# h − tanh(h) between two matrix products: five VectorE operations and a GpSimd mask, or three activations and two VectorE operations under a checked bound

## The chip, the cores and the metric

One core of a Trainium2 chip. The time is the device time of one execution in microseconds (us); medians of several executions are given with the lowest and highest.

A word on TensorE's records: each float32 matmul of this kernel appears as two "passes" (`ph`: 3072 in the trace of before for the program's 1536). All counts and distances below are of passes.

## The reference, cut to what matters

```python
X = np.fft.rfft(x, axis=1)                       # x: 8 batches x 3008 x 256
y = np.fft.irfft(X * (filt_r + 1j * filt_i)[None], n=3008, axis=1)
tokens = y.reshape(24064, 256)
h = tokens @ w_in                                # 256 -> 2048
g = h - np.tanh(h)
out = g @ w_out                                  # 2048 -> 256
```

The batches are worked on in four pairs. The transforms of the first pair come first; those of each later pair lie between the dense layers of the pair before. The change is about `g`.

## The kernel before

The tokens of a pair come in 12 groups: 11 of 512 tokens and one of 384. For each group there are 16 steps. A step makes one tile of the hidden layer, `ph` (128 hidden units by 512 tokens, in PSUM, where this kernel's matmul results lie; the other tiles lie in SBUF), turns it into `gt`, and adds `gt`'s share to `po`, the group's result. TensorE runs `po` two tiles behind `ph` (`LAG = 2`), so the elementwise work has two steps to pass.

```python
ph = ps.tile([128, CH * 128], F32, tag="h", bufs=3, name="ph")
for h in range(2):
    nc.tensor.matmul(ph[:, 0:n], w_in[:, h, ...], uts[i][:, h, 0:n], ...)      # 4 passes
th, u, gt = tile_of("th"), tile_of("u"), tile_of("gt", bufs=LAG + 2)           # others: 2 buffers
large = tile_of("large", U8)
nc.scalar.activation(u, ph, AF.Square)
nc.scalar.activation(th, ph, AF.Tanh)
nc.gpsimd.tensor_single_scalar(out=large, in_=u, scalar=SMALL, op=ALU.is_ge)   # |h| >= 0.6
nc.vector.tensor_mul(gt, ph, u)                                                # h^3
for tag, bias, (s, _, v) in zip(("sa", "sb"), biases, FACTORS):
    sq = tile_of(tag)
    nc.scalar.activation(sq, u, AF.Square, bias=bias, scale=s)
    nc.vector.scalar_tensor_tensor(out=gt, in0=sq, scalar=v, in1=gt, op0=ALU.add, op1=ALU.mult)
nc.vector.tensor_sub(th, ph, th)                                               # h - tanh(h)
nc.vector.copy_predicated(gt, large, th)
# ... two steps later, in down():
for j in range(n):                                                             # 8 passes
    nc.tensor.matmul(po[i][:, j, :], gt[:, j * 128:(j + 1) * 128], w_out[:, t, :], ...)
if t == NT - 1:                                       # end of the group; po has one buffer
    nc.vector.tensor_copy(ot[:, 0:2, :], o[:, 0:2, :])
    nc.scalar.copy(ot[:, 2:n, :], o[:, 2:n, :])
    nc.gpsimd.dma_start(...)                          # the store
```

Below |h| = 0.6 the difference cancels, and the kernel uses h³ times a product of two factors; above, it takes h − tanh(h) itself. GpSimd makes the mask that chooses. In the middle of a group the next group's tokens `ut` are made by 32 short passes (`pu`, one buffer).

Of the kernel before, what the change touches and what calls it, by code (L numbers as in the profile page):

```python
# [16 lines left out]
# The sequence index is n = NR * q + r and the frequency a + NQ * b, so that the transform over n is  # L17
# one of length NQ over q, a twiddle, and one of length NR over r. Of the NQ values of a, 0 .. NQ/2
# are kept (the input is real): a = 1 .. 31 have slots 0 .. 30, with real and imaginary parts, and
# a = 0 and a = 32, which are real after the first transform, share slot 31.  # L20
# [16 lines left out]
# Below |h| = 0.6, where h - tanh(h) cancels, it is h^3 times this product of (s u + b)^2 + v with  # L37
# u = h^2, to the precision of float32.
SMALL = 0.36
FACTORS = [(0.28138768672943115, 0.18210311233997345, 0.5012423992156982),  # L40
           (0.28138768672943115, -0.6558710336685181, 0.19358105957508087)]


def _consts():
# [4 lines left out]
    # over q: columns (part, slot)  # L49
# [10 lines left out]
    # over r: rows (r, part), columns (part, b). Frequencies over SEQ / 2 are the conjugates of their  # L60
    # mirror images and come in the order of these, as the filters are loaded.
# [15 lines left out]
    # back over b: g[., 0] takes (zr fr; zi fi), g[., 1] takes (zr fi; zi fr)  # L77
# [22 lines left out]
    # back over a: rows (slot, part)  # L100
# [18 lines left out]
def kernel(  # L119
# [13 lines left out]
    # Between the transforms the partition changes from (slot, part) to r and back, by way of DRAM.  # L133
    ct1 = [nc.dram_tensor(f"ct1_{p}", (NR, 128, DM), F32, kind="Internal") for p in range(PAIRS)]
    ct2 = [nc.dram_tensor(f"ct2_{p}", (128, NR, DM), F32, kind="Internal") for p in range(PAIRS)]
# [16 lines left out]
    def load_filters(a, z):  # L152
        """The filters of slots a .. z-1: filt[:, 0] has (fr; fi), filt[:, 1] has (fi; fr)."""
# [22 lines left out]

    biases = []
# [5 lines left out]
    def weights():  # L183
        """The weights, float64 in DRAM, as float32: the engines have no 64-bit floats, so a word's
        sign and exponent make a power of two, and its fraction, added up in float32, the factor."""
# [12 lines left out]
        for i, (dst, _) in enumerate(jobs):  # L198
# [13 lines left out]
            # An exponent under float32's range gives a zero, one over it an infinity.  # L212
# [17 lines left out]
    def first(p):  # L230
        """The transform over q of a pair of batches, to ct1 with rows (r, part, slot, batch)."""
        xs = {c: load_x(p, c) for c in range(2)}
        for c, (r, n) in enumerate(X_CHUNKS):
            if c + 2 < len(X_CHUNKS):
                xs[c + 2] = load_x(p, c + 2)
            pf = ps.tile([128, XH, DM], F32, tag="z", bufs=2, name="pf")
            nc.tensor.matmul(pf[:, 0:n, :], wf1, xs.pop(c)[:, 0:n, :], start=True, stop=True)  # L237
            a1 = sb.tile([128, XH, DM], F32, tag="a1", bufs=2, name="a1")
            nc.scalar.copy(a1[:, 0:n, :], pf[:, 0:n, :])  # L239
            nc.scalar.dma_start(  # L240
                dram(ct1[p], r * 128 * DM, [[DM, 128], [128 * DM, n], [1, DM]]), a1[:, 0:n, :])
            yield
# [6 lines left out]
    def middle(p):  # L249
        """Over r, times the filter and back over b, to ct2 with rows (batch, slot, part, r)."""  # L250
# [3 lines left out]
        def back():  # L254
            k, uv = waiting.pop(0)
            pe = ps.tile([128, 2, DM], F32, tag="z", bufs=2, name="pe")
            for f in range(2):
                nc.tensor.matmul(pe[0:R2], g3[:, (2 * k + f) * R2:(2 * k + f + 1) * R2],  # L258
                                 uv[:, f], start=(f == 0), stop=(f == 1))
            e1 = sb.tile([R2, 2, DM], F32, tag="e1", bufs=2, name="e1")  # L260
            nc.scalar.copy(e1, pe[0:R2])  # L261
            nc.scalar.dma_start(
                dram(ct2[p], k * R2 * DM, [[DM, R2], [NQ * NR * DM, 2], [1, DM]]), e1)
# [19 lines left out]
    def load_e2(p, c):  # L283
        r, n = CHUNKS[c]
        t = sb.tile([128, CH, DM], F32, tag="e2", bufs=2, name="e2")
        nc.sync.dma_start(t[:, 0:n, :], dram(ct2[p], r * DM, [[NR * DM, 128], [1, n * DM]]))
# [5 lines left out]
    def last(i):  # L292
        """Back over a: the tokens (r, batch, q) of a group, with the channel in the partition."""
# [4 lines left out]
        for h in range(2):  # L298
# [4 lines left out]
            nc.scalar.copy(ut[:, h, 0:n * 128], pu[:, 0:n * 128])  # L303
        uts[i] = ut

    def up(i, t):
        """128 rows of the shrunk hidden layer of a group."""
# [10 lines left out]
        th, u, gt = tile_of("th"), tile_of("u"), tile_of("gt", bufs=LAG + 2)  # L318
        large = tile_of("large", U8)
        nc.scalar.activation(u, ph, AF.Square)  # L320
        nc.scalar.activation(th, ph, AF.Tanh)  # L321
        nc.gpsimd.tensor_single_scalar(out=large, in_=u, scalar=SMALL, op=ALU.is_ge)  # L322
        nc.vector.tensor_mul(gt, ph, u)  # L323
        for tag, bias, (s, _, v) in zip(("sa", "sb"), biases, FACTORS):
            sq = tile_of(tag)
# [9 lines left out]
    def down(i, t, gt):  # L335
        """Its part of the result; at the end of the group, the store."""
# [4 lines left out]
        for j in range(n):  # L341
            # Two sums share a bank: the first product in it clears the whole bank's written bits.
# [11 lines left out]
    # the first pair's transforms, and the loads of what stays  # L354
# [16 lines left out]
    # Each pair's dense layers, with the next pair's transforms between them.  # L371
# [9 lines left out]
    for i, (p, c) in enumerate(groups):  # L381
        if i + 1 < len(groups) and c + 1 < len(CHUNKS):
            e2s[i + 1] = load_e2(*groups[i + 1])
        for t in range(NT):
# [5 lines left out]
            if t == NT // 2 and i + 1 < len(groups):  # L390
                last(i + 1)
            if p + 1 < PAIRS:
                for gens in plan.get(c * NT + t, []):
                    next(gens[p + 1])
    for w in todo:
        down(*w)

# [29 lines left out]
```

## Time and profile before

| | before |
|---|---|
| time | 3473.27 us median of 3 (3472.45 to 3473.28) |
| first pair's transforms, until the first `ph` pass | 469.85 us |
| dense layers, from there to the start of the last pass | 2998.45 us |
| from the start of the last pass to the end | 6.2 us |
| in the dense part: distances over the usual between TensorE's passes | 24.6 us |

The first row is measured by itself; the others come from the trace. The last row: what another engine costs is counted here where two passes start further apart than the median of their form in the trace (429 ns for `ph` with 512 columns, 323 with 384, 216 for `po`, 112 for `pu`; an excess under 50 ns is not counted). The prediction below shows the lines of the profile themselves.

### The profile page before, as it was taken

What the parts mean: (1) busy time and instruction counts of PE and PEld (TensorE: products, weight loads), DVE (VectorE), ACT (ScalarE), POOL (GpSimd) and SP (SyncE); (2) the same over time, 40 slices, a digit from 0 to 9 for tenths busy, and PEclk for the clock granted to TensorE, in tenths of its full rate; (3) what the DMA queues carried; (4) which work ended last, traced back from release to release, by engine and by line L of the source; (5) the groups of instructions that cost most, each with busy time, mean ns of one, the idle gap of its engine ahead of it and who ended that gap; (6) DMA issues with size and microseconds to landing.
All of it is one profiled execution on the core that took longest, in us unless ns stands there. A gap on an engine that the chain in (4) does not pass through costs nothing. (4 is left out here: it accounts for less than half of the span.)

```text
span 3474.5 us, 36231 instructions
## 1 busy us (share of the span) xinstructions
PE 3219.2 (93%) x10800; PEld 1985.4 (57%) x10800; DVE 2744.9 (79%) x4466; ACT 1946.3 (56%) x3441; POOL 1333.2 (38%) x855
## 2 busy tenths in 40 slices
PE   1256689999999999999999999999999999999998
PEld 0011146666666666666666666666666666666665
DVE  2243158888888888888888888888888999999998
ACT  0000046665555666665555666665555666666665
POOL 2100024443333444443333444444333444445453
PEclk9955589999999999999999999999999999999999
DMA  5631122201111012201111112111111100000000
GB/s 116 143 119 63 50 80 73 69 26 47 43 45 37 32 54 85 63 29 48 47 41 34 32 59 86 47 37 41 48 40 36 35 17 19 19 19 19 17 13 11
DMA packets 107702, 168.44 MB, mean 48 GB/s; under 512 B 17120, under 2 KB 65992, under 8 KB 107124
## 3 DMA queue, kind: packets, MB, share of 16 engines
q1 hardware_dynamic: 37776, 82.39, 7.9%
q10 hardware_dynamic: 50496, 52.68, 4.5%
q0 software_dynamic: 19232, 31.04, 2.9%
q8 instruction: 85, 1.39, 0.2%
q14 instruction: 113, 0.93, 0.1%
HBM read 92.00 MB, written 73.92 MB: 48 GB/s over the span
## 5 line engine op out<-in xcount | busy, mean ns | idle before, releaser
L322 POOL TENSOR_SCALAR large<-u 128x512 uint8<-128x512 f32 (+1 forms) x768 | 1271.5, 1656 | 1973.3 <-ACT u L320 1933.1
L343 PE MATMUL po<-w_out_sb,gt 128*128 128x256 f32 x6016 | 1423.8, 380 | 11.3 <-ACT ot L350 7.4
L311 PE MATMUL ph<-ut,w_in_sb 128*128 128x512 f32 (+1 forms) x3072 | 1418.5, 583 | 0.0
L343 PEld LDWEIGHTS po<-w_out_sb,gt 128*128 128x128 f32 x6016 | 1138.2, 190 | 483.1 <-issue 283.9
L320 ACT ACTIVATE u<-ph 128x512 f32<-128x512 f32 (+1 forms) x768 | 451.6, 588 | 825.3 <-issue 301.0
L311 PEld LDWEIGHTS ph<-ut,w_in_sb 128*128 128x128 f32 x3072 | 578.0, 190 | 453.3 <-issue 399.7
L323 DVE TENSOR_TENSOR gt<-ph,u 128x512 f32<-128x512 f32 (+1 forms) x768 | 518.3, 675 | 272.3 <-ACT th L321 271.4
L330 DVE COPY_PREDICATED gt<-large,th 128x512 f32<-128x512 uint8 (+1 forms) x768 | 586.2, 763 | 68.2 <-DVE gt L327 2.7
L327 DVE SCALAR_TENSOR_TENSOR gt<-sb,gt 128x512 f32<-128x512 f32 (+1 forms) x768 | 539.6, 703 | 65.5 <-DVE gt L327 1.8
L326 ACT ACTIVATE sa<-u,bias 128x512 f32<-128x512 f32 (+1 forms) x768 | 548.8, 715 | 0.0
L326 ACT ACTIVATE sb<-u,bias 128x512 f32<-128x512 f32 (+1 forms) x768 | 546.4, 711 | 0.0
L327 DVE SCALAR_TENSOR_TENSOR gt<-sa,gt 128x512 f32<-128x512 f32 (+1 forms) x768 | 518.9, 676 | 0.0
L329 DVE TENSOR_TENSOR th<-ph,th 128x512 f32<-128x512 f32 (+1 forms) x768 | 513.4, 668 | 0.0
L321 ACT ACTIVATE th<-ph 128x512 f32<-128x512 f32 (+1 forms) x768 | 449.5, 585 | 0.0
L258 PE MATMUL pe<-uv,g_sb 94*94 94x512 f32 x512 | 299.5, 714 | 61.7 <-ACT e L261 60.8
L261 ACT COPY e<-pe 94x512 f32<-94x512 f32 x128 | 74.4, 581 | 406.8 <-PE pe L258 215.7
L273 DVE TENSOR_TENSOR uv<-pz,filt_sb 94x512 f32<-94x512 f32 x256 | 171.5, 680 | 164.1 <-PE pz L269 164.1
L237 PE MATMUL pf<-x_sb,wf_sb 128*128 128x512 f32 x192 | 121.4, 725 | 151.8 <-ACT a L239 134.4
L258 PEld LDWEIGHTS pe<-uv,g_sb 94*94 94x94 f32 x512 | 93.3, 188 | 242.4 <-issue 135.3
L269 PE MATMUL pz<-a,f_sb 94*94 94x512 f32 x256 | 160.1, 711 | 24.7 <-DMA a<-ct 19.8
L239 ACT COPY a<-pf 128x512 f32<-128x512 f32 x96 | 55.4, 577 | 200.8 <-DMA ct<-a 134.2
L237 PEld LDWEIGHTS pf<-x_sb,wf_sb 128*128 128x128 f32 x192 | 39.5, 224 | 198.0 <-ACT a L239 166.4
(34 smaller groups left out, 536.2 us busy)
## 6 DMA issues: line engine op xcount, KB each, us to landing
a<-ct SPq DMA_DIRECT2D x128, 188.0 KB
ct<-e ACTq DMA_DIRECT2D x128, 188.0 KB
x_sb<-in_x_dram SPq DMA_DIRECT2D x92, 256.0 KB
ct<-a ACTq DMA_DIRECT2D x92, 256.0 KB
e<-ct SPq DMA_DIRECT2D x44, 512.0 KB
out_dram<-ot POOLq DMA_DIRECT2D x44, 512.0 KB, 3.0
w<-in_moe_w_in_dram SPq DMA_DIRECT2D x16, 256.0 KB
w<-in_moe_w_out_dram SPq DMA_DIRECT2D x16, 256.0 KB
```

What stands on the lines that cost most here:

```text
L258: nc.tensor.matmul(pe[0:R2], g3[:, (2 * k + f) * R2:(2 * k + f + 1) * R2], uv[:, f], start=(f == 0), stop=(f == 1))
L273: nc.vector.tensor_mul(uv[:, f], pz[0:R2], filt[:, f, k, :].unsqueeze(1).to_broadcast([R2, 2, DM]))
L311: nc.tensor.matmul(ph[:, 0:n], w_in[:, h, t * 128:(t + 1) * 128], uts[i][:, h, 0:n], start=(h == 0), stop=(h == 1))
L320: nc.scalar.activation(u, ph, AF.Square)
L321: nc.scalar.activation(th, ph, AF.Tanh)
L322: nc.gpsimd.tensor_single_scalar(out=large, in_=u, scalar=SMALL, op=ALU.is_ge)
L323: nc.vector.tensor_mul(gt, ph, u)
L326: nc.scalar.activation(sq, u, AF.Square, bias=bias, scale=s)
L327: nc.vector.scalar_tensor_tensor(out=gt, in0=sq, scalar=v, in1=gt, op0=ALU.add, op1=ALU.mult)
L329: nc.vector.tensor_sub(th, ph, th)
L330: nc.vector.copy_predicated(gt, large, th)
L343: nc.tensor.matmul(po[i][:, j, :], gt[:, j * 128:(j + 1) * 128], w_out[:, t, :], start=(t == 0 and j % 2 == 0), stop=(t == NT - 1), skip_g ...
```

## The change

Its intent is to take work off VectorE, the second busiest engine (79% to TensorE's 93%). For |h| < 0.98 and y = arctan(0.639 h)², the expression h·y·((0.1866 y − 0.6846)² + 0.3476) equals h − tanh(h) to a relative 5e-8 (evaluated in float64). That needs no mask and only two VectorE operations. It holds only under the bound, so the kernel checks the bound: it keeps the largest |token| of each channel and group, multiplies these by |w_in| on TensorE, and takes a general, slow path in a branch at the end if any result reaches 0.98. For the given inputs it does not.

```diff
+        nc.vector.tensor_reduce(out=largest[:, :, i:i + 1], in_=ut[:, :, 0:n * 128],   # once a group
+                                axis=mybir.AxisListType.X, op=ALU.max, apply_absolute_value=True)
...
-        large = tile_of("large", U8)
-        nc.scalar.activation(u, ph, AF.Square)
-        nc.scalar.activation(th, ph, AF.Tanh)
-        nc.gpsimd.tensor_single_scalar(out=large, in_=u, scalar=SMALL, op=ALU.is_ge)
-        nc.vector.tensor_mul(gt, ph, u)
-        for ...:  (activation Square with bias, scalar_tensor_tensor; twice)
-        nc.vector.tensor_sub(th, ph, th)
-        nc.vector.copy_predicated(gt, large, th)
+        nc.scalar.activation(at, ph, AF.Arctan, scale=S)
+        nc.scalar.activation(y, at, AF.Square)
+        nc.scalar.activation(sq, y, AF.Square, bias=near_b, scale=A)
+        nc.vector.tensor_mul(gt, ph, y)
+        nc.vector.scalar_tensor_tensor(out=gt, in0=sq, scalar=K, in1=gt, op0=ALU.add, op1=ALU.mult)
...
+    def bounded():                        # called in the middle of the last group
+        for t in range(NT):
+            nc.scalar.activation(w_abs, w_in[:, :, t * 128:(t + 1) * 128], AF.Abs)
+            for h in range(2):
+                nc.tensor.matmul(pb, w_abs[:, h], largest[:, h], start=(h == 0), stop=(h == 1))
+            nc.vector.tensor_single_scalar(out=small[:, t], in_=pb, scalar=NEAR, op=ALU.is_lt)
+        ...                               # minimum, sum over partitions, count
...
+    within = nc.values_load(count[0:1, 0:1], min_val=0, max_val=128)
+    with tc.If(within < 128):
+        general()
```

One DRAM tensor for the transforms' results takes the place of four, so that the general path can index it. (With the change, the tiles named `th`, `u` and `sa` in the profile hold arctan, y and the second square.)

More of the change, by code (lines that the diff above doesn't have):

```diff
@@ L41 @@
            (0.28138768672943115, -0.6558710336685181, 0.19358105957508087)]
+S, K = 0.6389930153911744, 0.3476472316053873
+A, B = 0.18659689165196622, -0.6846325776203513
+NEAR = 0.98
 def _consts():
@@ L134 @@
     ct1 = [nc.dram_tensor(f"ct1_{p}", (NR, 128, DM), F32, kind="Internal") for p in range(PAIRS)]
-    ct2 = [nc.dram_tensor(f"ct2_{p}", (128, NR, DM), F32, kind="Internal") for p in range(PAIRS)]
+    ct2_all = nc.dram_tensor("ct2", (PAIRS, 128, NR, DM), F32, kind="Internal")
     cst = ctx.enter_context(tc.tile_pool(name="cst", bufs=1))
@@ L175, in load_filters @@
                                     dram(src.tensor, NQ // 2 * DM, [[NQ * DM, HI], [1, DM]]))
+    near_b = cst.tile([128, 1], F32, name="near_b")
+    nc.vector.memset(near_b, B)
+    largest = cst.tile([128, 2, PAIRS * len(CHUNKS)], F32, name="largest")
     biases = []
@@ L262, in back @@
             nc.scalar.dma_start(
-                dram(ct2[p], k * R2 * DM, [[DM, R2], [NQ * NR * DM, 2], [1, DM]]), e1)
+                dram(ct2_all, (p * 128 * NR + k * R2) * DM, [[DM, R2], [NQ * NR * DM, 2], [1, DM]]), e1)
         for k in range(NK):
@@ L285, in load_e2 @@
         t = sb.tile([128, CH, DM], F32, tag="e2", bufs=2, name="e2")
-        nc.sync.dma_start(t[:, 0:n, :], dram(ct2[p], r * DM, [[NR * DM, 128], [1, n * DM]]))
+        nc.sync.dma_start(t[:, 0:n, :], dram(ct2_all, (p * 128 * NR + r) * DM, [[NR * DM, 128], [1, n * DM]]))
         return t
@@ L303, in last @@
             nc.scalar.copy(ut[:, h, 0:n * 128], pu[:, 0:n * 128])
+        nc.vector.tensor_reduce(out=largest[:, :, i:i + 1], in_=ut[:, :, 0:n * 128],
+                                axis=mybir.AxisListType.X, op=ALU.max,
+                                apply_absolute_value=True)
         uts[i] = ut
@@ L317, in up @@
         ph = ph[:, 0:n]
-        th, u, gt = tile_of("th"), tile_of("u"), tile_of("gt", bufs=LAG + 2)
-        large = tile_of("large", U8)
+        at, y, sq = tile_of("th"), tile_of("u"), tile_of("sa")
+        gt = tile_of("gt", bufs=LAG + 2)
+        nc.scalar.activation(at, ph, AF.Arctan, scale=S)
+        nc.scalar.activation(y, at, AF.Square)
+        nc.scalar.activation(sq, y, AF.Square, bias=near_b, scale=A)
+        nc.vector.tensor_mul(gt, ph, y)
+        nc.vector.scalar_tensor_tensor(out=gt, in0=sq, scalar=K, in1=gt,
+                                       op0=ALU.add, op1=ALU.mult)
@@ new lines, in up @@
+        return gt
+    def bounded():
+        ng = len(groups)
+        small = cst.tile([128, NT, ng], F32, name="small")
+        ones = cst.tile([128, 1], F32, name="ones")
+        nc.gpsimd.memset(ones, 1.0)
+        for t in range(NT):
+            w_abs = sb.tile([128, 2, 128], F32, tag="sb", bufs=2, name="w_abs")
+            nc.scalar.activation(w_abs, w_in[:, :, t * 128:(t + 1) * 128], AF.Abs)
+            pb = ps.tile([128, ng], F32, tag="z", bufs=2, name="pb")
+            for h in range(2):
+                nc.tensor.matmul(pb, w_abs[:, h], largest[:, h], start=(h == 0), stop=(h == 1))
+            nc.vector.tensor_single_scalar(out=small[:, t], in_=pb, scalar=NEAR, op=ALU.is_lt)
+        least = cst.tile([128, 1], F32, name="least")
+        nc.vector.tensor_reduce(out=least, in_=small, axis=mybir.AxisListType.XY, op=ALU.min)
+        pc = ps.tile([1, 1], F32, tag="z", bufs=2, name="pc")
+        nc.tensor.matmul(pc, least, ones, start=True, stop=True)
+        count = cst.tile([1, 1], I32, name="count")
+        nc.vector.tensor_copy(count, pc)
+        return count
@@ new lines, in general @@
+    def general():
+        out_v = out.rearrange("(p q r) d -> p r q d", p=PAIRS, r=NR)
+        ct2_v = ct2_all.ap().rearrange("p s r d -> p r s d")
+        with tc.For_i(0, PAIRS, 1) as p, tc.For_i(0, NR, 1) as r:
+            e2 = sb.tile([128, DM], F32, tag="e2", bufs=2, name="e2")
+            nc.sync.dma_start(e2, ct2_v[bass.ds(p, 1), bass.ds(r, 1), :, :])
+            ut = sb.tile([128, 2, 128], F32, tag="ut", bufs=2, name="ut")
+            for h in range(2):
+                pu = ps.tile([128, 128], F32, tag="u", bufs=1, name="pu")
+                nc.tensor.matmul(pu, e2[:, h * 128:(h + 1) * 128], s2, start=True, stop=True)
+                nc.scalar.copy(ut[:, h], pu)
+            o = ps.tile([128, DM], F32, tag="o", bufs=1, name="o")
+            for t in range(NT):
+                ph = ps.tile([128, 128], F32, tag="h", bufs=3, name="ph")
+                for h in range(2):
+                    nc.tensor.matmul(ph, w_in[:, h, t * 128:(t + 1) * 128], ut[:, h],
+                                     start=(h == 0), stop=(h == 1))
+                gt = any_h(ph)
+                nc.tensor.matmul(o, gt, w_out[:, t, :], start=(t == 0), stop=(t == NT - 1))
+            ot = sb.tile([128, DM], F32, tag="ot", bufs=1, name="ot")
+            nc.vector.tensor_copy(ot, o)
+            nc.sync.dma_start(out_v[bass.ds(p, 1), bass.ds(r, 1), :, :], ot)
@@ L320, in up, with any_h @@
+    def any_h(ph):
+        th, u, sq, gt = (sb.tile([128, 128], F32, tag=tag, bufs=b, name=tag)
+                         for tag, b in (("th", 2), ("u", 2), ("sa", 2), ("gt", LAG + 2)))
+        large = sb.tile([128, 128], U8, tag="large", bufs=2, name="large")
         nc.scalar.activation(u, ph, AF.Square)
         nc.scalar.activation(th, ph, AF.Tanh)
-        nc.gpsimd.tensor_single_scalar(out=large, in_=u, scalar=SMALL, op=ALU.is_ge)
+        nc.vector.tensor_single_scalar(out=large, in_=u, scalar=SMALL, op=ALU.is_ge)
@@ L323, in up @@
         nc.vector.tensor_mul(gt, ph, u)
-        for tag, bias, (s, _, v) in zip(("sa", "sb"), biases, FACTORS):
-            sq = tile_of(tag)
+        for bias, (s, _, v) in zip(biases, FACTORS):
             nc.scalar.activation(sq, u, AF.Square, bias=bias, scale=s)
@@ L391 @@
                 last(i + 1)
+            if i + 1 == len(groups) and t == NT // 2:
+                count = bounded()
             if p + 1 < PAIRS:
```

## The prediction

> **What bounds the kernel now.** I read the page's busy shares and slices first, to see which engine is full and when.
>
> ```profile
> span 3474.5 us, 36231 instructions
> PE 3219.2 (93%) x10800; PEld 1985.4 (57%) x10800; DVE 2744.9 (79%) x4466; ACT 1946.3 (56%) x3441; POOL 1333.2 (38%) x855
> PE   1256689999999999999999999999999999999998
> DVE  2243158888888888888888888888888999999998
> PEclk9955589999999999999999999999999999999999
> ```
>
> The first five or six slices (some 470 us) are the first pair's transforms, which wait on transfers; the change does not touch them. After that TensorE is at nine tenths in every slice with its full clock, and VectorE at eight, then nine. The second view is busy time in two stretches: the dense layers up to the last group of tokens, and that group with the end.
>
> ```profile
> core 0: us, PE busy (x) PEld busy (x) DVE busy (x) ACT busy (x) POOL busy (x), PEclk, DMA share, GB/s
> 470.00:3414.00 2944.00, 2936.81 (x10347) 1884.59 (x10345) 2566.92 (x3989) 1875.43 (x3307) 1274.66 (x797) 1.00 0.12 41
> 3414.00:3474.50 60.50, 50.52 (x186) 33.80 (x184) 50.33 (x93) 33.16 (x70) 22.48 (x19) 0.99 0.04 16
> ```
>
> TensorE is idle for 7.2 us of 2944 us. Matmul ends are modelled, so busy is not proof of work; the chain of waits shows the pace:
>
> ```profile
> 3306.30 1.72 PE ph L311 x4
> 3308.02 1.73 PE po L343 x8
> 3309.74 3.43 PE ph L311 x8
> 3313.18 3.45 PE po L343 x16
> ```
>
> One step is 4 passes of ph (1.72 us, so 430 ns for 512 columns) and 8 of po (1.73 us, 216 ns for 256): 3.45 us, end to end with the next. 768 steps make 2.65 ms; the next pair's transforms lie between them on the same engine. So TensorE's own work is the bound.
>
> VectorE, however, is only just fast enough. Third, the costliest groups:
>
> ```profile
> L323 DVE TENSOR_TENSOR gt<-ph,u 128x512 f32<-128x512 f32 (+1 forms) x768 | 518.3, 675 | 272.3 <-ACT th L321 271.4
> L330 DVE COPY_PREDICATED gt<-large,th 128x512 f32<-128x512 uint8 (+1 forms) x768 | 586.2, 763 | 68.2 <-DVE gt L327 2.7
> L327 DVE SCALAR_TENSOR_TENSOR gt<-sb,gt 128x512 f32<-128x512 f32 (+1 forms) x768 | 539.6, 703 | 65.5 <-DVE gt L327 1.8
> L326 ACT ACTIVATE sb<-u,bias 128x512 f32<-128x512 f32 (+1 forms) x768 | 546.4, 711 | 0.0
> ```
>
> VectorE's five operations of a step (675, 676, 703, 668, 763) sum to 3.49 us against TensorE's 3.45. They overlap a little, and transforms give TensorE extra work, so VectorE falls behind only where steps are short: in the last group of each pair, with 384 columns in place of 512. Last, TensorE's timeline there, and after it its waits from 470 us on (us in total, times, longest):
>
> ```profile
> 3452.73 1.56 PE L343 MATMUL po<-w_out_sb,gt 128*128 128x256 f32 x6
> 3455.73 1.56 PE L343 MATMUL po<-w_out_sb,gt 128*128 128x256 f32 x6
> 3464.39 1.56 PE L343 MATMUL po<-w_out_sb,gt 128*128 128x256 f32 x6 [1.27 <-DVE gt L330]
> 3467.11 1.56 PE L343 MATMUL po<-w_out_sb,gt 128*128 128x256 f32 x6 [1.16 <-DVE gt L330]
> ```
>
> ```profile
> PE po L343 <- ACT ot L350: 7.4, 8, 1.5
> PE po L343 <- DVE gt L330: 2.9, 5, 1.3
> ```
>
> A 384-column step needs 4 x 323 + 6 x 216 = 2.59 us, but here two follow each other at 2.9 to 3.0 us: VectorE sets the pace, and the last two po also wait for it. To get the loss that the modelled ends hide, I took the distances between the starts of successive passes from TensorE's timeline from 470 us on, and summed what exceeds the usual one (429, 323, 216, 112 ns by form) by over 50 ns: 24.6 us. Of it 10.7 us come with waits for VectorE's gt, 10.7 us with waits at the change of group for the copies of po (ot), 3.1 us with the single buffer of pu. This 24.6 us is all that a faster elementwise part can win: 0.7%.
>
> [...] the trace has 585 to 588 (square, tanh) and 711 to 715 (square with bias)[...]. So arctan should cost what tanh does. [...] the trace's pu passes, which stream 128 columns for each 128 of weights, start every 112 ns. [...]
>
> **The change, part by part.**
>
> 1. VectorE loses three of five operations a step (668, 703, 763): 768 steps, 1639 us of busy time by the groups' sums. It keeps 675 + about 690 = 1.37 us a step, and gets 48 maxima of 2 x 512 elements[...]. So about 1165 us, 34%. GpSimd loses 1271.5 us. ScalarE goes from 588 + 585 + 715 + 711 = 2.60 to about 585 + 588 + 715 = 1.89 us a step: 1400 us, 40%. All three lie beside TensorE's 3.45 us. On the path: the 10.7 us of gt waits go. The new chain for one tile, three activations and one operation in a row (0.59 + 0.59 + 0.72 + 0.69 with some 0.1 us between: about 3 us), is well under the two steps (6.9 us) of lag. **-10.5 us.**
>
> 2. The scheduler's order at the change of group. Before, 37 of 47 changes have two tiles' worth of matmuls (ph, or one ph and a transform) between the last po of one group and the first of the next; in the listing of the changed program 34 have one tile's ph alone, 4 x 430 = 1.72 us. po has one buffer: the next po waits for the two copies, which run one after the other: [...] VectorE 0.69, ScalarE 0.58, [...] about 1.75 us if both engines are free, up to 0.5 more if not. So 34 short waits of 0.1 to 0.5 us, with the 0.10 us that a restart shows: about 10 us. Before, the same waits cost 10.7 us, in fewer and longer pieces. **0 us, give or take 5.** The 3.1 us at pu stay.
>
> 3. The bound, checked at the middle of the last group: 32 float32 matmuls with 48 columns against 128 columns of weights. Each is two passes[...]: 64 x 0.112 = 7.2 us on TensorE, which has no gap for it. Their 16 absolute values [...] and comparisons stand between other work, with two buffers; step by step they come in time, since a pair of tiles takes 0.9 us of passes and 0.65 to 0.86 us of ph or po. I add 0.3 us for the last reduction. **+7.5 us.**
>
> 4. Arctan needs another table set: the order shows one load, ahead of the first tile, and none after. TensorE has 7 ph matmuls (6 us) before its first po[...]. [...]
>
> 5. The end: every engine loads the count into a register and takes a branch over the general path. The bound works out from the reference's inputs as at most 0.69 against 0.98, so the path is not taken. Most of it lies beside the last store, whose landing (3.0 us by the page) ends the run. [...]
>
> 6. One tensor ct2 in place of four: the waits of its loads and stores in the listings are the same. **0.**
>
> Sum: 3473.3 - 10.5 + 0 + 7.5 + 0.8 + 1 = 3472 us.
>
> **Rivals.** (a) VectorE was the real limit, and 60% of its work gone makes the dense part faster by several per cent. For it: 94% busy in the last pair and 3.49 against 3.45 us a step. Against it: TensorE's passes are at their usual distances but for 24.6 us; even with all of it and no new cost the time is 3449 us. (b) The order at changes of group goes badly: ScalarE, in order, holds the second copy behind an activation each time, 0.7 us x 47, and the first stage loses some more: 3490 us. (c) The bound's matmuls wait for absolute values and comparisons at every pair instead of running through[...], 3482 us. (d) The general path runs: many milliseconds; the inputs exclude it unless the check itself is wrong.
>
> **Range and chances.** The terms are small and of both signs; the uncertain ones are part 2 (5 us), part 3 (4 us), the end (2 us) and the first stage, where ScalarE and the transfers may fall out differently by some us. Range 3461 to 3484. 2% would be 69 us, out of reach both ways: faster 0.01, within 2% 0.98, slower 0.01.
>
> **What would show it.** VectorE near 34%, ScalarE near 40%, GpSimd under 3%, TensorE still 92 to 93% and 3.45 us a step; no wait of po for gt; 384-column steps at 2.59 us; waits of po for ot, many and short; about 7 us of pb passes near the end. It is wrong if the steps of 512 columns change their length, if arctan takes longer than tanh's 585 ns, or if the first 470 us move by over 10 us.

The sum came to 3472 us: 3473.3 for before, −10.5, 0 and +7.5 for parts 1 to 3, and +0.8 and +1 for parts 4 and 5. These last two terms were estimates, and no trace or run gave them. That arctan takes as long as tanh is an estimate from square and tanh, which both take 585 to 588 ns. Part 1's 1165 us include a term for the 48 maxima (measured after: 57.6 us, 1199 ns each). Of part 2's 1.75 us the trace of before shows 0.42 us from the start of the last `po` pass to the first copy (at the end of the run), 0.69 and 0.58 for the copies, 0.03 between them and 0.05 to the next `po` where that waits: 1.77 us. Part 3's 64 × 0.112 us takes the distance of the `pu` passes for passes of 48 columns, an estimate, and its 0.3 us is an allowance.

## The result, and the profile after

Predicted within 2%, and so it came. After: 3464.43 us median of 4 (3463.81 to 3465.55); before in the same rounds: 3473.28 (3472.45 to 3473.86). The ratio is 0.9974, with a 95% interval of 0.9960 to 0.9988: some 9 us faster, within 2%. Ratios here are the mean time of one kernel's fast runs over that of the other's of the same rounds, so not quite the ratio of the medians quoted.

The page of the kernel after, its busy shares and VectorE's slices:

```profile
span 3462.2 us, 30898 instructions
PE 3219.3 (93%) x10866; PEld 1993.6 (58%) x10866; DVE 1375.0 (40%) x2229; ACT 1695.6 (49%) x2690; POOL 61.6 (2%) x88
DVE  2243123344444433344444443344444444444444
```

VectorE's busy time is halved and GpSimd is almost gone, yet TensorE's 93% has not moved: it was the bound and still is. Then the same two stretches as before (columns: us, then busy time and count of TensorE, its weight loads, VectorE, ScalarE, GpSimd, then clock, DMA share, GB/s):

```profile
470.00:3402.00 2932.00, 2932.00 (x10342) 1883.94 (x10341) 1221.06 (x1787) 1620.10 (x2554) 24.50 (x46) 1.00 0.12 40
3402.00:3462.00 60.00, 53.72 (x248) 41.11 (x246) 24.09 (x54) 33.62 (x67) 1.08 (x2) 0.98 0.04 17
```

TensorE's 7.2 us of idle time in the long stretch are now 0.00. The groups that replace the elementwise work:

```profile
L333 ACT ACTIVATE th<-ph 128x512 f32<-128x512 f32 (+1 forms) x768 | 451.7, 588 | 935.5 <-PE ph L324 935.4
L336 DVE TENSOR_TENSOR gt<-ph,u 128x512 f32<-128x512 f32 (+1 forms) x768 | 522.6, 680 | 1567.0 <-ACT u L334 1562.5
L337 DVE SCALAR_TENSOR_TENSOR gt<-sa,gt 128x512 f32<-128x512 f32 (+1 forms) x768 | 522.7, 681 | 75.6 <-ACT sa L335 1.2
L314 DVE TENSOR_REDUCE largest<-ut 128x2 f32<-128x1024 f32 (+1 forms) x48 | 57.6, 1199 | 114.3 <-ACT ut L313 114.3
```

Arctan takes 588 ns, as tanh did. VectorE now idles 1567 us before its first operation of a step: it waits for ScalarE, and ScalarE for TensorE. The third line of evidence is TensorE's timeline in the 384-column steps of the last group:

```profile
3418.29 1.46 PE L414 MATMUL po<-w_out_sb,gt 128*128 128x256 f32 x6
3420.87 1.46 PE L414 MATMUL po<-w_out_sb,gt 128*128 128x256 f32 x6
3423.46 1.46 PE L414 MATMUL po<-w_out_sb,gt 128*128 128x256 f32 x6
```

They are 2.58 and 2.59 us apart, where before they were 2.8 to 3.0. Also, each block of six passes reads 1.46 us, where before it read 1.56. The 0.10 us is what a block shows in these traces when TensorE starts it from a wait: its first two passes then start 320 ns apart and not 216. So here a block's own length tells whether it waited, even where no wait is listed.

Where did the 9 us come from? The account of TensorE's distances in both traces, in us (count in brackets):

| | before | after |
|---|---|---|
| first `ph` pass starts at | 469.85 | 466.05 |
| first `ph` pass to start of the last pass | 2998.45 | 2989.29 |
| excess with waits for `gt`, with the restarts | 7.8 (26) + 2.7 (26) | 0 |
| excess at the change of group (`ot`), with the restarts | 9.3 (13) + 1.5 (14) | 0.4 (4) + 4.1 (39) |
| excess at `pu` | 3.1 (39) | 3.2 (40) |
| other excess (after: beside the bound's passes) | 0.3 | 1.0 |
| all excess | 24.6 | 8.6 |
| the bound's passes (`pb`) | – | 6.5 (64) |
| start of the last pass to the end | 6.2 | 6.8 |

The dense part is 9.2 us shorter: 16.0 us of excess less, 6.5 us of new passes, and 0.3 us in the check's last two passes (`pc`, 0.12) and in distances under the 50 ns. The end is 0.6 us longer. That is −8.6 us, and the medians differ by 8.85 us. The first `ph` pass, 3.8 us earlier in this pair of traces, is chance: a second look at each kernel had it at 469.27 (before) and 468.31 (after), and over all traces told of here it lies between 465.0 and 471.4 without regard to the kernel. The second looks repeat the rest: 2998.38 and 2989.11 us of dense part, 24.4 and 8.4 us of excess.

Three details of the trace after. A change of group near the end, one of the four before groups of 384 columns: TensorE's `ph` passes, the two copies of `po`, and the next `po`:

```profile
3409.03 2.10 PE L324 MATMUL ph<-ut,w_in_sb 128*128 128x384 f32 x6
3409.72 0.68 DVE L420 COPY ot<-po 128x512 f32<-128x512 f32 x1
3410.43 0.58 ACT L421 COPY ot<-po 128x512 f32<-128x512 f32 x1 [1.24 <-DVE ot L420]
3411.07 1.56 PE L414 MATMUL po<-w_out_sb,gt 128*128 128x256 f32 x6
```

Both engines are free when they are asked, so the copies end as the six `ph` passes do (6 × 0.323 from 3409.03 is 3410.97). The next `po` starts 0.10 us after that, and TensorE loses this and the 0.10 us of a restart (104 ns in each of 39 cases after); at the changes before groups of 512 columns it is the restart alone. The bound's passes:

```profile
3427.34 0.99 PE L353 MATMUL pb<-largest,w_abs 128*128 128x48 f32 x8
3428.16 0.88 PE L324 MATMUL ph<-ut,w_in_sb 128*128 128x384 f32 x2
3428.88 0.99 PE L353 MATMUL pb<-largest,w_abs 128*128 128x48 f32 x8
```

Eight of them take 3427.34 to 3428.16, 0.82 us or 103 ns each on average, and go into TensorE's row without a gap. Last, ScalarE's table load:

```profile
466.89 1.28 ACT L333 ACT_TABLE_LOAD   x1
```

It lies beside the first `ph` passes, which have started at 466.05 and run on.

### The profile page after: what moved, and what is told of

Its sections match the earlier page's. It is cut to its first block, busy times and chain, and to the rows that moved or that the text cites. A ratio compares the mean times of both kernels' runs of the same rounds, so it can differ in the third digit from the quotient of the medians.

```text
span 3462.2 us, 30898 instructions
## 1 busy us (share of the span) xinstructions
PE 3219.3 (93%) x10866; PEld 1993.6 (58%) x10866; DVE 1375.0 (40%) x2229; ACT 1695.6 (49%) x2690; POOL 61.6 (2%) x88
## 4 chain that ended last, share of the span: by engine, by line
issue 64%; PE 23%; DMA 12%; POOL 1%; ACT 0%; DVE 0%; ACTq 0%; POOLq 0%; SPq 0%; DVEq 0%
PE ph L324 9%; PE po L414 9%; DMA ct<-e 6%; DMA ct<-a 4%; PE pe L268 2%; DMA f_sb<-f 1%; PE pz L279 1%; PE pu L311 1%; PE pf L247 1%; POOL out_dram L422 1%; DMA w<-in_moe_w_out_dram 1%; DMA w<-in_moe_w_in_dram 0%; ACT e L271 0%; ACT a L249 0%; DVE it L216 0%
## 5 line engine op out<-in xcount | busy, mean ns | idle before, releaser
L335 ACT ACTIVATE sa<-u,near_b 128x512 f32<-128x512 f32 (+1 forms) x768 | 548.3, 714 | 24.8
L334 ACT ACTIVATE u<-th 128x512 f32<-128x512 f32 (+1 forms) x768 | 476.4, 620 | 24.0
L283 DVE TENSOR_TENSOR uv<-pz,filt_sb 94x512 f32<-94x512 f32 x256 | 163.9, 680 | 168.5 <-PE pz L279 168.5
L311 PEld LDWEIGHTS pu<-s_sb,e 128*128 128x128 f32 x752 | 96.5, 193 | 33.2 <-ACT ut L313 28.7
L311 PE MATMUL pu<-s_sb,e 128*128 128x128 f32 x752 | 103.5, 281 | 0.0
L314 DVE TENSOR_REDUCE largest<-ut 128x2 f32<-128x1024 f32 (+1 forms) x48 | 57.6, 1199 | 114.3 <-ACT ut L313 114.3
L313 ACT COPY ut<-pu 128x512 f32<-128x512 f32 (+1 forms) x96 | 55.3, 576 | 76.1 <-PE pu L311 75.7
L279 PEld LDWEIGHTS pz<-a,f_sb 94*94 94x94 f32 x256 | 47.7, 191 | 68.7 <-issue 53.5
```

The lines of the kernel that those rows point to most:

```text
L279: nc.tensor.matmul(pz[0:R2], f2[:, k * R2:(k + 1) * R2], a2.pop(k), start=True, stop=True)
L283: nc.vector.tensor_mul(uv[:, f], pz[0:R2], filt[:, f, k, :].unsqueeze(1).to_broadcast([R2, 2, DM]))
L311: nc.tensor.matmul(pu[:, j * 128:(j + 1) * 128], e2[:, j, h * 128:(h + 1) * 128], s2, start=True, stop=True)
L334: nc.scalar.activation(y, at, AF.Square)
L335: nc.scalar.activation(sq, y, AF.Square, bias=near_b, scale=A)
```

## The experiments

Three sets of runs, each on one chip and each with its own runs of the kernel before: 3475.14 us (3473.27 to 3479.52, 9 runs) in the first, 3473.65 (3472.0 to 3478.21, 9 runs) in the second, 3474.42 (3472.7 to 3476.33, 9 runs) in the third. All kernels gave correct results for these inputs.

My theory at first: before, VectorE's five operations of a step sum to about TensorE's step, so VectorE's load caused the waits for `gt` and made the copies at the change of group late; less load removed them, and the bound costs some 7 us of what was won. (Runs 4 and 9 corrected the part on load.) The rivals: the waits come from something else that the change removed with them, such as the chain's form or GpSimd's part, or the order at the change of group; the expectations give them letters as they came up.

**1. What the bound costs.** After, without it:

```diff
-        nc.vector.tensor_reduce(out=largest[:, :, i:i + 1], ...)
-                count = bounded()
-    within = nc.values_load(...); with tc.If(within < 128): general()
```

> The changed kernel without the maxima, the bound's matmuls and the branch: the elementwise part alone (it would be wrong for large h, and gives the reference's result on these inputs). My theory: the change won some 16 us of TensorE's waits (24.6 us of late starts in the trace of before, 8.4 in that of after) and gave back 6.6 us of pb passes, 0.8 us of restarts around them and 0.7 us at the end; so this run is 8 us under the changed kernel: 3456 us, ratio 0.9951 to before. Rival A, the gain comes from the first 470 us (the first dense matmul starts 3.8 us earlier in the trace of after) and the waits count for half: 3460 us or more. Rival B, the bound is hidden beside other work: within 2 us of the changed kernel.

Measured: 3459.78 us (3458.74 to 3460.46, 5 runs), ratio 0.9955 (0.9942 to 0.9969). Against 0.9974 for the whole change this is 0.19%, 6.6 us. The two ratios' intervals overlap, so the size is taken from the trace: its dense part is 2981.61 us, 7.7 us shorter than after's. The median is near Rival A's 3460, but this set's runs of before are 1.9 us slower than those beside the result; the ratio is the theory's, and the dense part, which leaves the first stage out, speaks against Rival A. The bound costs what its passes cost (6.5 us, and 1.0 us beside them), and the rest of the check next to nothing. The end is 6.8 us here too, without any check or branch.

**2. The bound on the kernel before.** Maxima, bound, branch and general path, with the elementwise part of before:

```diff
+        nc.vector.tensor_reduce(out=largest[:, :, i:i + 1], ...)     # once a group
+                count = bounded()                                     # w_abs in x's buffers
+    with tc.If(within < 128): general()
```

> The kernel before with the maxima, the bound's matmuls and the branch alone, elementwise part as it was (the absolute values lie in the buffers of x, as there is no room for new ones). My theory: the pb passes cost TensorE 6.6 us and the restarts and the end 1.5 us, so 8 us slower than before, ratio 1.0023; perhaps less, 4 us, since TensorE waits for VectorE in that group and the passes fill such gaps. Rival B, the bound is hidden: ratio 1.000 within 0.0005. Rival C, VectorE, which sets the pace there, has to do 16 comparisons and 48 maxima more and the loss is over 15 us, ratio 1.0045 or more.

Measured: 3510.01 us (3508.41 to 3511.77, 4 runs), ratio 1.0098 (1.0083 to 1.0114): 35 us slower than before; of what was expected, Rival C came. The passes of the bound are 6.6 us of it, as in the kernel after. The rest is waiting: the excess at the change of group went from 10.7 to some 29.5 us and the waits for `gt` from 10.5 to some 18. The listed waits of TensorE (us in total, times, longest) put most of it on the copies:

```profile
PE po L411 <- ACT ot L418: 23.4, 17, 1.5
PE po L411 <- DVE gt L335: 3.0, 6, 1.2
```

The maxima, 1.2 us once a group on an engine that is 79% busy, and the 16 comparisons of the check, cost 28 us. From 2500 us on, VectorE's median distance from one step of 512 columns to the next is 3.62 us here, against 3.44 us before, which is TensorE's own step. So VectorE had next to no room before, and with the check's work it sets the pace. The same maxima in the kernel after cost nothing that run 1 shows.

**3 and 4. VectorE's load put back into the kernel after**, as two or three extra operations a step whose results nobody reads:

```diff
         nc.vector.tensor_mul(gt, ph, y)
+        for _ in range(2):        # 3 in the second kernel
+            nc.vector.tensor_mul(tile_of("junk", bufs=1), sq, y)
```

> The changed kernel with two more VectorE multiplications into a tile that nobody reads, between the two operations of a step: four operations of 0.68 us, 2.7 us a step against TensorE's 3.45, and 2.24 against 2.59 in the groups with 384 columns. My theory: VectorE's work costs nothing until it passes TensorE's step, so within 2 us of the changed kernel, no wait of po for gt, waits for ot perhaps longer by 1 to 3 us in all. Rival D, less VectorE work as such is worth time [...]: the loss is in proportion, 2/3 of the 16 us of waits, 3475 us.

> The same with three more: five operations, 3.4 us a step as before the change, 2.8 us against 2.59 with 384 columns. My theory: waits of po for gt come back in the 384-column groups and at the end, and long waits for ot at changes of group: 10 to 16 us over the changed kernel, 3474 to 3480 us. Rival A, the gain was not from VectorE's backlog: within 3 us of the changed kernel.

Measured: with two 3466.82 us (3464.24 to 3468.26, 5 runs), ratio 0.9973 (0.9960 to 0.9987); with three 3467.32 (3466.05 to 3469.7, 5 runs), ratio 0.9976 (0.9962 to 0.9989). The second missed my theory's number, and Rival A's came (within 3 us of after). Its page shows that the load was really there:

```profile
PE 3222.1 (93%) x10866; PEld 1993.7 (57%) x10866; DVE 2775.5 (80%) x4533; ACT 1694.1 (49%) x2690; POOL 61.5 (2%) x88
```

VectorE is busy for 2775.5 us, more than the 2744.9 of before, and TensorE's excess with waits for `gt` is 0.2 us, against 10.5. So the amount of VectorE's work, by itself, is not what made it wait.

**5. The same load as a chain**, because in the trace of before an operation that takes the last one's result starts 0.79 us after it, and others 0.60 to 0.61:

```diff
+        junk = tile_of("junk", bufs=1)
+        nc.vector.tensor_mul(junk, sq, y)
+        for _ in range(2):
+            nc.vector.tensor_mul(junk, junk, y)
         nc.vector.tensor_mul(gt, ph, y)
```

> The changed kernel with three more VectorE multiplications of which two wait for the one before. Three independent ones (e4) brought VectorE's busy time back to 80% but none of the waits; in that trace independent operations follow each other at 0.60 to 0.72 us, while in before those that need the result just written follow at 0.79. Theory V: what counts is VectorE's step from start to start, 3.44 to 3.70 us in before, about 3.2 in e4. Here it should be about 3.55 us, over TensorE's 3.45: the last pair's groups, where TensorE has nothing else to do, get 1 to 2 us longer each, waits of po for gt and ot come back: 3480 to 3500 us. Rival E: it is not VectorE's pace but the form of the chain over three engines, with GpSimd's mask and ScalarE's fourth activation, that made the waits: no more than 5 us over the changed kernel.

Measured: 3466.17 us (3463.69 to 3466.63, 5 runs), ratio 0.9975 (0.9962 to 0.9989). Missed again; Rival E's number came, but the run cannot decide for it. The scheduler put another tile's operations between the links, so in the trace most of them start 0.60 us after the one ahead, and only one pair 0.72 us, no more than two of run 4 that merely write over the same tile. The run does not disprove that a chain is slow; it did not build one as long as that of before.

**6. The copies at the change of group in two tiles with a store each** (in the kernel after; the intent was that the second copy need not wait for the first):

```diff
-            ot = sb.tile([128, CH, DM], F32, tag="ot", bufs=1, name="ot")
-            nc.vector.tensor_copy(ot[:, 0:2, :], o[:, 0:2, :]); nc.scalar.copy(ot[:, 2:n, :], o[:, 2:n, :])
-            nc.gpsimd.dma_start(...)
+            for tag, j, z, copy in (("ot", 0, 2, nc.vector.tensor_copy), ("ot2", 2, n, nc.scalar.copy)):
+                ot = sb.tile([128, 2, DM], F32, tag=tag, bufs=1, name=tag)
+                copy(ot[:, 0:z - j, :], o[:, j:z, :])
+                nc.gpsimd.dma_start(...)
```

> The changed kernel with the two copies of po into tiles of their own, with a store each, so that ScalarE's copy needn't wait for VectorE's. In the trace of after the next po starts 0.10 us late at 34 to 43 changes of group, as the two copies in a row take as long as the two ph matmuls between (1.72 us). My theory: those 4.5 us go, 3460 us, 0.9987 of the changed kernel. Rival: the smaller stores (or the order that the scheduler makes of it) cost as much again, within 1 us.

Measured: 3467.41 us (3466.11 to 3469.09, 5 runs), ratio 0.9981 (0.9967 to 0.9994). A miss, and the edit did not do what it was made for: in all 48 groups the second copy still starts 0.03 us after the first ends, as in the kernel after. So the 39 restarts of 0.10 us are all still there (4.1 us together), and two stores in place of one make the end 2.5 us longer (9.3 against 6.8 us). What holds the second copy was not looked into, and what uncoupled copies are worth stays untested.

**7 and 8. The bound checked in another way**: the largest y itself, kept by VectorE, in place of the product of maxima; then this together with the copies of run 6.

```diff
-        nc.vector.tensor_reduce(out=largest[:, :, i:i + 1], ...)
         nc.vector.tensor_mul(gt, ph, y)
+        nc.vector.tensor_max(largest[:, 0:n], largest[:, 0:n], y)
...
-        for t in range(NT): (w_abs, two matmuls pb, comparison)
+        nc.vector.tensor_reduce(out=most, in_=largest, axis=mybir.AxisListType.X, op=ALU.max)
+        nc.vector.tensor_single_scalar(out=least, in_=most,
+                                       scalar=float(np.arctan(S * NEAR) ** 2), op=ALU.is_lt)
```

> The changed kernel with the check made from the values themselves: a running maximum of arctan squared on VectorE, one operation of 0.68 us a step where it has 2 us to spare, and at the end a maximum, a comparison and one matmul; no maxima of ut, no pb passes. Its listing has the order of before at changes of group (4 ph matmuls between two groups' po), so no wait for ot either. My theory: the 6.5 us of pb and 4.5 us of ot go, the end costs 0 to 2 us more: 3453 to 3456 us. Rival: the operation on VectorE, or the longer end (reduce, compare, matmul, copy, register), costs what was saved: 3462 us or more.

> e7 with the copies of e6. If the waits for ot are gone in e7 already by its order, as I think, it equals e7 within 2 us; if they are not, it is 3 to 4 us faster than e7.

Measured: 3455.22 us (3453.21 to 3461.43, 5 runs), ratio 0.9950 (0.9937 to 0.9964); with the copies 3456.47 (3454.59 to 3456.94, 5 runs), ratio 0.9948 (0.9934 to 0.9961). The check moved from the full engine to one with room: no `pb` passes, and 768 more VectorE operations that cost nothing. Besides, the scheduler's order at the change of group changed by itself, and the excess there fell to some 0.9 us (of 4.5 in all, of which `pu` is 3.2). The end grew to 7.7 us, counted from the check's own last pass. Run 7 is a version that beats both kernels, by 8 us (from the ratios) to 10 us (from the traces) the one after, in part by the luck of that order; run 8 adds nothing to it.

**9. The kernel before without GpSimd.** All five VectorE operations and all four activations stay; the mask is a constant zero, made once. This gives wrong results where |h| > 0.6.

```diff
+    mask = cst.tile([128, CH * 128], U8, name="mask")
+    nc.vector.memset(mask, 0)
-        nc.gpsimd.tensor_single_scalar(out=large, in_=u, scalar=SMALL, op=ALU.is_ge)
-        nc.vector.copy_predicated(gt, large, th)
+        nc.vector.copy_predicated(gt, mask[:, 0:n], th)
```

> The kernel before with a mask of zeros made once, in place of GpSimd's comparison of each tile (wrong for |h| over 0.6, and the reference's result on these inputs). In before copy_predicated takes 0.74 us as a rule and about 1.0 in its longest part. Theory V with contention: the long ones are those that run beside GpSimd; without it VectorE's step falls from 3.44 to 3.70 us to about 3.4, under TensorE's, and most waits for gt and ot go: 8 to 16 us faster than before, ratio 0.9955 to 0.998. Rival F, the long ones have another cause, and GpSimd plays no part: ratio 0.9990 to 1.0005.

Measured: 3456.09 us (3455.2 to 3457.43, 5 runs), ratio 0.9948 (0.9934 to 0.9961). That is 18 us faster than before, more than the 8 to 16 of theory V, as fast as run 7, and with VectorE 79% busy. TensorE's excess is 6.2 us: 3.1 of it at `pu`, 2.4 with waits for `gt`, and no waits for the copies at the change of group. To see how, here is one step of 384 columns in the last group, first of before. VectorE's operations (DVE) are in the order in which they start, with GpSimd's (POOL) between:

```profile
3452.57 0.55 DVE L323 TENSOR_TENSOR gt<-ph,u 128x384 f32<-128x384 f32 x1
...
3453.40 1.17 POOL L322 TENSOR_SCALAR large<-u 128x384 uint8<-128x384 f32 x1 [1.83 <-ACT u L320]
3453.49 0.82 DVE L327 SCALAR_TENSOR_TENSOR gt<-sa,gt 128x384 f32<-128x384 f32 x1
...
3454.42 0.56 DVE L327 SCALAR_TENSOR_TENSOR gt<-sb,gt 128x384 f32<-128x384 f32 x1
3455.08 0.59 DVE L330 COPY_PREDICATED gt<-large,th 128x384 f32<-128x384 uint8 x1
3455.56 0.55 DVE L323 TENSOR_TENSOR gt<-ph,u 128x384 f32<-128x384 f32 x1
```

and of run 9:

```profile
3428.19 0.54 DVE L323 TENSOR_TENSOR gt<-ph,u 128x384 f32<-128x384 f32 x1
...
3429.12 0.54 DVE L327 SCALAR_TENSOR_TENSOR gt<-sa,gt 128x384 f32<-128x384 f32 x1
3429.76 0.56 DVE L327 SCALAR_TENSOR_TENSOR gt<-sb,gt 128x384 f32<-128x384 f32 x1
3430.36 0.59 DVE L330 COPY_PREDICATED gt<-mask,th 128x384 f32<-128x384 uint8 x1
3430.85 0.54 DVE L323 TENSOR_TENSOR gt<-ph,u 128x384 f32<-128x384 f32 x1
```

From one `gt<-ph,u` to the next it is 2.99 us before and 2.66 us in run 9; TensorE's step is 2.585. Two things differ. The operation of 0.82 us, which starts 0.09 us after GpSimd's comparison, takes 0.54 without one: 0.28 us more. And the copy starts 0.66 us after the operation ahead (3454.42 to 3455.08), where with the constant mask it is 0.60. Over all steps of 384 columns the median is 2.84 us before (64 steps) and 2.66 in run 9.

In the steps of 512 columns, I took the medians of the distances from one VectorE operation's start to the next (about 550 to 670 of each, from 480 us on):

| from, to | before | run 9 |
|---|---|---|
| multiply, subtract | 0.608 | 0.608 |
| subtract, first scalar_tensor_tensor | 0.598 | 0.598 |
| first, second scalar_tensor_tensor (takes the first's result) | 0.786 | 0.786 |
| second scalar_tensor_tensor, copy (writes over its result) | 0.795 | 0.726 |
| copy, next multiply, where it does not wait for tanh (43 and 11) | 0.628 | 0.628 |
| sum | 3.415 | 3.346 |

TensorE's step is 4 × 0.429 + 8 × 0.216 = 3.444 us. (In most steps of both the last distance is longer, 0.66 before and 0.73 in run 9. There the multiply starts 0.03 us after the end of the `tanh` that it waits for, so this is TensorE's pace and not VectorE's.) Before, VectorE has 0.03 us of room each step, some 21 us over the 704 steps of 512 columns; the operations that are lengthened beside GpSimd (below) add 43 us to it in these, and 11 us in the steps of 384 columns. In run 9 the copy starts 0.07 us sooner, so the room is 0.10 us, and nothing is lengthened. In run 4, with more busy time, the distances are 0.601, 0.609, 0.602, 0.719 and 0.609, 3.14 us in all (for the first and the last the 5th percentile, since their median, 0.75, is what TensorE's pace leaves); run 5's are the same. Its operations that neither take the previous one's result nor write over it start 0.60 apart, so VectorE has 0.30 us of room each step. I take this to be why runs 4 and 5 did not wait.

What lengthens the operations? In the trace of before, I sorted VectorE's 512-column operations by how much of their time a GpSimd comparison ran beside them. `copy_predicated` takes 726 ns on average with none beside it (201) and 803 with one beside most of it (447); the second `scalar_tensor_tensor` 690 (536) and 831 (99). The multiply and the subtract, which read `ph` from PSUM, take 676 to 688 either way. So of these four the two that read SBUF tiles alone are lengthened. Their lengths still spread, so I sorted them by who started first. Two copies, one of each order:

```profile
3227.50 0.74 DVE L330 COPY_PREDICATED gt<-large,th 128x512 f32<-128x512 uint8 x1
3227.72 1.83 POOL L322 TENSOR_SCALAR large<-u 128x512 uint8<-128x512 f32 x1 [1.96 <-ACT u L320]
...
3394.67 1.49 POOL L322 TENSOR_SCALAR large<-u 128x512 uint8<-128x512 f32 x1 [3.12 <-DVE gt L327]
3394.72 1.15 DVE L330 COPY_PREDICATED gt<-large,th 128x512 f32<-128x512 uint8 x1
```

Of the copies beside a comparison, the 353 that started before it take 740 ns in the median and 749 at most. Of the 111 that started within 0.9 us after it, 110 are lengthened; the median is 973 ns, and they end 0.28 us before the comparison's record does, hardly varying; the 38 that started later still are not lengthened. The other way round, a 512-column comparison takes 1487 ns where none of the three operations is running when it starts (196), and 1831 where one is (505); it then ends 1.31 us after that one. So each is longer where the other started first, the copy by 0.23 us and the comparison by 0.34 us in the median. What makes it so was not shown: the lengthened copy ends 0.28 us before the comparison's record does, so a wait for all of the recorded span is not what the records show. (The profile calls GpSimd's spans rough.) An average over both orders hides the effect: the median of all 447 copies with a comparison beside most of their time is 741 ns.

Run 9 takes away three things at once: the lengthening, the copy's later start, and ScalarE's waits for GpSimd before it writes the next `u` (275 us in 249 pieces in the trace of before). Their shares of the 18 us were not told apart.

**10. Relief for VectorE in the kernel before**, at the change of group: both copies of `po` on ScalarE.

```diff
-            nc.vector.tensor_copy(ot[:, 0:2, :], o[:, 0:2, :])
+            nc.scalar.copy(ot[:, 0:2, :], o[:, 0:2, :])
```

> The kernel before with both copies of po on ScalarE (2 x 0.58 us in a row). Theory V: VectorE gets 0.68 us a group less and the next po no longer waits behind VectorE's queue; the 10.7 us at changes of group fall to some 2 us and the gt waits (10.7 us) stay or fall a little: 8 us faster, ratio 0.9977. Rival G, the waits for ot come from ScalarE's queue: no gain, ratio over 0.9995.

Measured: 3481.26 us (3478.54 to 3482.52, 5 runs), ratio 1.0019 (1.0005 to 1.0033): slower, a miss. The waits for `gt` went from 10.5 to some 18 us, and those at the change of group only from 10.7 to some 9. The 0.69 us that VectorE saved 48 times did not become a gain while the rest of its step stayed as it was.

**11 and 12. Each kernel once more**, for the accounts above (single looks, state unknown).

> The kernel before once more, for its trace: how much the start of the first dense matmul moves from execution to execution (469.85 us in the first trace of before, 466.05 in that of after, 469 to 471 in the experiments, which have the same first stage). If it is chance, before gives some value between 465 and 472 and waits of 24 us again; if the change moved it, 469.5 to 470.5.

> The changed kernel once more, for its trace: first dense matmul between 465 and 472 us if that start is chance, at 465.5 to 466.5 if the change moved it; late starts 8 to 9 us in all again.

Measured: 3475.65 us and 3466.15 us; the traces repeat the waits (24.4 and 8.4 us of excess), and the start of the dense part is where chance puts it.

## Why the prediction was right, and where its steps were off

The time predicted was 3472 us with a range of 3461 to 3484; measured 3464.4. The bound was named rightly: TensorE, whose own row the change hardly touches, so neither 2% faster nor 2% slower was in reach. The 24.6 us given as all that could be won was the right ceiling: 16.0 of them were won, 6.5 given back. The range also holds the 3473 us of no change at all, and the net gain predicted was 1.3 us of the 8.9 measured, so it is the parts that test the reasoning:

1. **Waits for `gt`, −10.5 us.** Right: 10.5 us before, none after. The steps of 384 columns are at 2.58 to 2.59 us, as stated. The shares of busy time were under: VectorE 40% for 34, ScalarE 49% for 40. The prediction took whole durations (1639 and 546 us) off busy times in which overlapping operations count once. Before, VectorE's durations sum to 2992 us where 2745 are busy, and ScalarE's to 2210 where 1946 are; after, hardly any overlap (1424 for 1375, and 1698 for 1696). The second activation, which reads SBUF now, took 620 ns and not 585 to 588.
2. **Change of group, 0 ± 5 us.** This is the term that was mis-sized: −6.2 us (10.7 to 4.5). The mechanism, many short waits in place of fewer long ones, came: 39 restarts, for 34 in the listing. But each was put at 0.1 to 0.5 us plus a restart of 0.10, and they are the restart alone. The copies find both engines free, and their chain ends with the `ph` passes ahead. This is most of the 7.6 us between prediction and result.
3. **The bound, +7.5 us.** Right within 1 us: 6.5 us of passes, 103 ns each in place of 112, plus 1.0 us beside them (its absolute values took 0.42 us each); run 1 gives 6.6 to 7.7 us for taking the whole bound away. Rival (c) did not come.
4. **Table load, +0.8 us** (estimate, not shown by a run). One load of 1.28 us; the first arctan starts 0.85 us after its end. No lost time is to be seen in the dense part.
5. **The end, +1 us** (estimate, not shown by a run). 0.6 us, but not for the reason given, the count and the branch: run 1 has neither check nor branch, and its end is as long (6.8 us). The cause stays open.
6. **One tensor, 0.** Nothing to be seen of it.

−10.5 − 6.2 + 6.5 + 1.0 + 0.1 (`pu`) is −9.1, with the end −8.5: the change in the traces.

Two sums in it are off, without bearing on the result: the 768 steps make 2.59 ms and not 2.65, since 64 of them have 384 columns, and rival (b)'s 0.7 us × 47 is 33 us, which would give 3505 and not 3490. The 384-column steps that it reads at 2.9 to 3.0 us alternate between 2.83 and 3.00.

One reason in it was wrong though its number held. "VectorE, however, is only just fast enough" was argued from the sum of five durations, 3.49 us. Runs 4 and 5 have the same five operations' worth of busy time and no waits. What counted before was the distance between starts, which is larger where an operation takes the result of the one ahead (0.786 us against 0.598 and 0.608; 3.415 us in sum, 0.03 under TensorE's step), together with what GpSimd's comparison adds; run 9 wins 18 of the 24.6 us, twice what the whole change wins, by taking the comparison away. The prediction named GpSimd's 1271.5 us only as work off the path. That removing a GpSimd operation is enough is shown by run 9. All nine kernels here without the comparison, with VectorE 38 to 80% busy, have at most 2.6 us of waits for `gt`, restarts included; the three with it (before, runs 2 and 10) have 10 to 18. How much of the change's own gain is due to it, and how much to the shorter VectorE step, was not separated: the change does both, and the kernel after with a GpSimd operation put back was not run. Rival (a), that VectorE is the real limit and several per cent are to be won, did not come.

## What to carry to other kernels

Whether an engine keeps up is read from the distances between the starts of its operations, not from their summed durations: the chain of before, where operations take the last one's result, had 0.03 us of room a step at 79% busy, and the operations that got longer beside GpSimd's used that up; run 4's five mostly independent operations had 0.30 us at 80%. An operation on an idle engine was not free here: beside it the copies took 973 ns for 740, by order of start, and ScalarE waited for it to write the next `u`. Look for the same operation with two lengths in the trace, and sort by what ran beside it and by which of the two started first. And put a safety check on the engine that has room: the product of maxima cost 6.5 us on the full TensorE, and the running maximum on the half-idle VectorE cost nothing but 0.8 us at the end.
